# Attention, two expert layers on one core: pooled v is put into its blocks by TensorE in place of on-chip transfers

## The chip, the cores and the metric

One core of a Trainium2 chip runs the whole program. The metric is the device time of one execution in microseconds (us). The profile is one further execution of the same program, with its own time.

## What is computed

The reference, cut to what matters here:

```python
batch, n_heads, seq, head_dim = (8, 8, 576, 64)        # q, k, v: [8, 8, 576, 64]

def _attn_ref(q, k, v):
    pool = 8
    Sp = S // pool                                      # 72 pooled rows
    k_p = k.reshape(B, H, Sp, pool, D).mean(axis=3)
    v_p = v.reshape(B, H, Sp, pool, D).mean(axis=3)
    scores = scale * np.matmul(q, k_p.transpose(0, 1, 3, 2))
    scores = scores - np.max(scores, axis=-1, keepdims=True)
    attn = np.exp(scores)
    attn = attn / (np.sum(attn, axis=-1, keepdims=True) + 1e-09)
    return np.matmul(attn, v_p)

x = attn_out.transpose(0, 2, 1, 3).reshape(B * S, H * D)   # 4608 tokens of 512
x = _moe_ref(x=x, **moe_kwargs)      # the best of 8 experts for each token, 512 -> 1024 -> 512
return _moe2_ref(x=x, **moe2_kwargs) # RMS norm, gated layer 512 -> 1536 -> 512
```

## The kernel before

The program has three parts, one after the other: the attention, the expert layer in slots of 256 tokens, and the gated layer. The change lies in the attention alone.

**Tiles.** The 4608 queries are cut into 36 tiles of 128 rows: four groups (`m`) of nine. In a group the tiles 0 to 3 belong to batch 2m, 4 to 7 to batch 2m+1, and the ninth, the mixed tile, takes the last 64 queries of both. For each tile `n` of the loop at the end of the quoted code the same five steps are written out: `emit_pt(n)` turns the exponentials of the scores with TensorE (line 384, tile `pt`) and ScalarE copies them to `ptsb` (L386); `emit_qt(n + 3)` turns the queries (L348, `pq`, copied by ScalarE to `qt`); `emit_sc(n + 2)` multiplies them with the pooled keys `kbd` (L360, `sc`) and VectorE takes the maximum and subtracts; `emit_av(n)` multiplies with the pooled values (L394 or L402, `av`), VectorE divides into the output tile `x` (L421, L423), and SyncE stores it to DRAM (L426, `x_d`). The pool of output tiles, `x_p`, has three buffers, so tile n writes the buffer of tile n - 3, whose store must have landed.

**Two forms of the last product.** Tiles listed in `PLAIN` use the pooled values as they lie, in `vau`: 72 pooled rows, 8 heads of 73 columns (64 values, a one for the sum, 8 router logits). Each head needs a turn of 72 columns and a product of 73 columns, eight of each. The other tiles use blocks, `vbd`: the 4 x 72 rows of four heads are cut into three pieces of 96 rows, each with the two heads that meet in it side by side (146 columns). That is six turns and six products a tile.

**Filling the blocks.** For every batch `rows_v` and `prep_vg` fill `vau` (ScalarE L287, VectorE L322). Then `place_v` copies it into the three buffers of `vbd` in turn with six transfers from SBUF to SBUF on SyncE's queue (L330), 48 in all. Everything outside the blocks' filled cells is zero and was cleared once by GpSimd at the start (L692).

**What sets the order.** Each engine runs its instructions in the order written. The table `ORDER` and the list `E1` say at which tile, and at which of the places "a" to "e" between the five steps, a load, a pooling step or a placement stands. All plain transfers are issued by SyncE, in order: loads of q, k and v, stores of x, placements, and from tile 25 on the first expert's weights (`st`, L158 and L161), which ScalarE casts (L143) between the copies of the tiles. The build gives the transfers eight completion counters in turn, so each waits for the eighth before it to land. Loads take their buffers from a ring of 36 (`wtile`), and so does `ptsb` in a `PLAIN` tile. GpSimd pools (L241, L242 for k, L265 to L267 for v) and scatters the routing order (`ord_d`, L478).

Of the kernel before, what the change touches and what calls it, by code (L numbers as in the profile page):

```python
# [9 lines left out]
F32 = mybir.dt.float32  # L10
# [10 lines left out]
NP = 72  # L21
# [32 lines left out]

CW = [19, 30, 35, 35, 47]

PLAIN = (0, 1, 2, 3, 4, 5, 6, 9)


C_ID, C_IE, C_OFF, C_P, C_PK, C_TRI, C_TOK, C_END = 0, 128, 136, 144, 147, 211, 339, 375  # L60
# [21 lines left out]
def fused(ctx: ExitStack, tc: tile.TileContext, q, k, v, moe_w_gate, moe_w1, moe_w2,  # L82
          w_gate, w_val, w_out, rms_g, cst, out):
    nc = tc.nc
# [14 lines left out]
    ident = cc[:, C_ID:C_ID + 128]  # L99
# [39 lines left out]
    def wtile(dt, name):  # L139
        return wp.tile([128, 1024], dt, tag="w", name=name)  # L140
# [38 lines left out]
    ps = rctx.enter_context(tc.tile_pool(name="ps_a", bufs=1, space=PSUM))  # L179
    actx = ExitStack()  # L180
# [4 lines left out]
    at4 = actx.enter_context(tc.tile_pool(name="at4", bufs=1))  # L185
    at_p = actx.enter_context(tc.tile_pool(name="at", bufs=2))
    kv1 = actx.enter_context(tc.tile_pool(name="kv1", bufs=1))
    x_p = actx.enter_context(tc.tile_pool(name="xo", bufs=3))

    kbd = [at4.tile([128, 4, 2, NP], F32, name=f"kbd{i}") for i in range(3)]  # L190
    vbd = [at4.tile([96, 2, 3, 146], F32, name=f"vbd{i}") for i in range(3)]
    vau = [at4.tile([NP, H, 73], F32, name=f"vau{i}") for i in range(2)]
    lgs = sm1.tile([128, 36, E], F32, name="lgs")

# [128 lines left out]

    def place_v(b):

        va, vb = vau[b % 2], vbd[b % 3]
        v4 = va.rearrange("s (g h) n -> s g h n", g=2)
        for h, c, side, p0, s0, n in ((0, 0, 0, 0, 0, 72), (1, 0, 1, 72, 0, 24), (1, 1, 0, 0, 24, 48),
                                      (2, 1, 1, 48, 0, 48), (2, 2, 0, 0, 48, 24), (3, 2, 1, 24, 0, 72)):
            nc.sync.dma_start(out=vb[p0:p0 + n, :, c, 73 * side:73 * side + 73], in_=v4[s0:s0 + n, :, h])  # L330

    def tiles_of(m):
        return [(m, i) for i in range(9)]
# [42 lines left out]
    def emit_pt(n):  # L376
        pe = pes.pop(n).rearrange("p a h s -> p (a h s)")
        pt = [pa.tile([128, 4, 128], F32, tag=f"p{g}", name="pt") for g in range(2)]
        if n in PLAIN:
            sb, np_, nb = wtile(F32, "ptsb").rearrange("p (g c t) -> p g c t", g=2, c=4), NP, 4  # L380
# [8 lines left out]
    def emit_av(n, between=None):  # L389
        m, i = tl[n]  # L390
        sb = pts.pop(n)
        av = pav.tile([128, 2, 512], F32, tag="av", name="av")
        for h in range(H) if n in PLAIN else ():
            nc.tensor.matmul(av[:, h // 4, 73 * (h % 4):73 * (h % 4) + 73], lhsT=sb[0:NP, h // 4, h % 4],  # L394
                             rhs=vau[(2 * m + i // 4) % 2][:, h])
        for g in range(2) if n not in PLAIN else ():

# [209 lines left out]
    for name, soon, later in ORDER:  # L607
        for m in range(1, 4):
            i = soon if m == 1 else later
            plan(9 * (m - 1) + i // 5, "abcde"[i % 5], lambda f=steps[name[:-1]], b=2 * m + int(name[-1]): f(b))  # L610
    for i, w, f, x in ((E1[0], 0, sum_rows, ("k", 1, 2, nc.vector)), (E1[1], 0, sum_rows, ("k", 1, 3, nc.vector)),
                       (E1[2], 0, place_v, (0,)), (E1[3], 0, rows_k, (1,)),
                       (E1[4], 0, sum_rows, ("v", 1, 2, nc.vector)), (E1[5], 0, sum_rows, ("v", 1, 3, nc.vector)),
                       (E1[6], 0, rows_v, (1,)), (E1[7], 0, prep_vg, (1,)),
                       (E1[8], 0, place_v, (1,)), (E1[9], 0, prep_k, (GB,))):
        plan(i // 5, "abcde"[i % 5], lambda f=f, x=x: f(*x))
# [71 lines left out]
    sum_rows("v", 0, 3, nc.gpsimd)  # L688
    for z in range(2):
        nc.vector.tensor_copy(out=wg[64 * z:64 * z + 64, :, z], in_=wgl[64 * z:64 * z + 64])  # L690
    for t in kbd[1:] + vbd:
        nc.gpsimd.memset(t, 0.0)  # L692
    emit_qt(1)
    keep_warm(3)
# [348 lines left out]
    for s in range(SURE):  # L1043
# [11 lines left out]
        a = unit_steps(s, 0)  # L1055
# [169 lines left out]
```

## Time and profile before

| | us |
|---|---|
| median of 3 runs | 1744.29 (1741.7 to 1753.03) |
| the profiled execution | 1744.8 |
| span of its instructions | 1743.0 |
| the attention's tiles, about | 40 to 276 of the span |
| expert layer, about | 276 to 820 |
| gated layer, about | 820 to 1743 |

TensorE is busy 94% of the span and its mean granted clock is 0.965. The two later parts are nearly full of matmuls; the gaps are in the attention. The page's chain that ended last reaches back only to 814 us, and so says nothing of the part that is changed; for that part the waits and the order of time are read.

### The profile page before, as it was taken

To read this page: it belongs to the slowest core of one execution; us is meant where nothing else is said; L and a number is where in the kernel's file an instruction comes from. 1 tells how busy PE (TensorE), PEld (TensorE's weight loads), DVE (VectorE), ACT (ScalarE), POOL (GpSimd) and SP (SyncE) were. 2 spreads that over 40 slices of the span, in tenths; PEclk is the share of its full clock that TensorE was granted. 3 is DMA by queue.
4 is the path that set the end of the run, shared out by engine and by line. 5 is a ranking of instruction groups with operands and counts; after the bars stand their busy time and mean duration, and the time that the engine had idled before them with its cause. 6 is when DMAs were issued, how large, how long until landed. Compare 5 with 4: busy or idle time off the path is not lost.

```text
span 1743.0 us, 31176 instructions
## 1 busy us (share of the span) xinstructions
PE 1630.7 (94%) x11306; PEld 1497.9 (86%) x11307; DVE 874.7 (50%) x2087; ACT 522.6 (30%) x1186; POOL 428.1 (25%) x470
## 2 busy tenths in 40 slices
PE   7967777999899998998999999999999999999998
PEld 5867766888788887898999999999999999999997
DVE  5756765678865768522434333334433333443322
ACT  2433341243432444322222222222222222222211
POOL 5654554455643536211200000000000000000000
PEclk8877888999999999999999999999999999999999
DMA  9987872557763754313700000000000000000000
GB/s 184 237 138 172 157 124 81 195 164 237 240 197 122 244 171 164 105 37 130 271 9 19 25 26 25 25 8 18 25 25 25 25 25 7 19 25 13 13 13 13
DMA packets 116881, 163.51 MB, mean 94 GB/s; under 512 B 51280, under 2 KB 70864, under 8 KB 116704
## 3 DMA queue, kind: packets, MB, share of 16 engines
q1 hardware_dynamic: 104992, 125.38, 26.8%
q0 software_dynamic: 11712, 35.91, 6.1%
q8 instruction: 94, 1.54, 0.4%
q14 instruction: 83, 0.68, 0.1%
HBM read 116.85 MB, written 43.06 MB: 92 GB/s over the span
## 4 chain that ended last, share of the span: by engine, by line
PE 50%; DMA 2%; issue 1%; POOL 0%; POOLq 0%; ACT 0%
PE g L1131 11%; PE g L1132 11%; PE g L1130 11%; PE po L1152 6%; PE po L1153 6%; PE po L1151 6%; DMA rl<-scr 1%; PE px L1011 1%; DMA rh<-scr 1%; DMA out_dram<-o,tk 0%; POOL rh L1100 0%; POOL rl L1100 0%; POOLq L1219 0%; ACT o L1154 0%; POOLq L1100 0%
## 5 line engine op out<-in xcount | busy, mean ns | idle before, releaser
L1131 PE MATMUL g<-xl,rh 128*128 128x256 f32 x1088 | 303.0, 278 | 0.0
L1132 PE MATMUL g<-xh,rl 128*128 128x256 f32 x1088 | 302.9, 278 | 0.0
L1130 PE MATMUL g<-xh,rh 128*128 128x256 f32 x1088 | 302.7, 278 | 0.0
L1155 POOL DMA_INDIRECT out_dram<-o,tk x36 | 34.8, 968 | 792.1 <-ACT o L1154 709.2
L1131 PEld LDWEIGHTS g<-xl,rh 128*128 128x128 f32 x1088 | 204.3, 188 | 0.0
L1130 PEld LDWEIGHTS g<-xh,rh 128*128 128x128 f32 x1088 | 204.1, 188 | 0.0
L1132 PEld LDWEIGHTS g<-xh,rl 128*128 128x128 f32 x1088 | 204.0, 187 | 0.0
L493 PE MATMUL p<-xh,w1h 128*128 128x256 f32 x672 | 191.7, 285 | 8.1 <-DVE hl L498 6.1
L494 PE MATMUL p<-xl,w1h 128*128 128x256 f32 x672 | 190.0, 283 | 0.7 <-DVE xl L530 0.7
L495 PE MATMUL p<-xh,w1l 128*128 128x256 f32 x672 | 189.6, 282 | 0.0
L1135 DVE SCALAR_TENSOR_TENSOR th<-th,g 128x256 f32<-128x256 f32 x216 | 91.0, 421 | 192.5 <-ACT th L1134 191.5
L1016 DVE SCALAR_TENSOR_TENSOR xl<-px,gt,xh 128x256 fp32r<-128x256 f32 x68 | 31.4, 482 | 263.5 <-ACT xh L1015 263.5
L1130 PE MATMUL g<-xh,uh 128*128 128x256 f32 x544 | 152.7, 281 | 0.0
L1131 PE MATMUL g<-xl,uh 128*128 128x256 f32 x544 | 151.5, 278 | 0.0
L1132 PE MATMUL g<-xh,ul 128*128 128x256 f32 x544 | 151.5, 278 | 0.0
L143 ACT CAST ah<-th 128x256 fp32r<-128x256 f32 x216 | 87.9, 407 | 203.5 <-DVE th L1136 203.5
L1134 ACT ACTIVATE th<-g 128x256 f32<-128x256 f32 x216 | 82.8, 383 | 207.4 <-PE g L1132 207.4
L144 DVE TENSOR_TENSOR al<-th,ah 128x256 fp32r<-128x256 f32 x216 | 92.0, 426 | 102.2 <-ACT ah L143 101.7
L1152 PE MATMUL po<-rl,ah 128*128 128x512 f32 x360 | 142.3, 395 | 0.1
L1151 PE MATMUL po<-rh,ah 128*128 128x512 f32 x360 | 142.2, 395 | 0.0
L1153 PE MATMUL po<-rh,al 128*128 128x512 f32 x360 | 142.2, 395 | 0.0
L493 PEld LDWEIGHTS p<-xh,w1h 128*128 128x128 f32 x672 | 127.7, 190 | 13.1 <-DVE hl L498 7.3
(259 smaller groups left out, 3607.0 us busy)
## 6 DMA issues: line engine op xcount, KB each, us to landing
st<-in_moe_w_dram SPq DMA_DIRECT2D x64, 512.0 KB
y_d<-ys SPq DMA_DIRECT2D x39, 256.5 KB
y<-y_d SPq DMA_DIRECT2D x18, 513.0 KB
v<-in_v_dram SPq DMA_DIRECT2D x32, 288.0 KB
x_d<-x SPq DMA_DIRECT2D x32, 260.0 KB
q<-in_q_dram SPq DMA_DIRECT2D x32, 256.0 KB
scr<-uh SPq DMA_DIRECT2D x13, 512.0 KB
scr<-ul SPq DMA_DIRECT2D x13, 512.0 KB
```

What stands on the lines that cost most here:

```text
L143: nc.scalar.copy(out=hi, in_=src)
L144: eng.tensor_tensor(out=lo, in0=src, in1=hi, op=ALU.subtract)
L493: nc.tensor.matmul(a, lhsT=w1h[d][:, fs], rhs=xh[:, d], start=d == 0, stop=False)
L494: nc.tensor.matmul(a, lhsT=w1h[d][:, fs], rhs=xl[:, d], start=False, stop=False)
L495: nc.tensor.matmul(a, lhsT=w1l[d][:, fs], rhs=xh[:, d], start=False, stop=d == 3)
L1130: nc.tensor.matmul(g[:, j], lhsT=wh[:, sl], rhs=hi[:, d], start=d == 0, stop=False)
L1131: nc.tensor.matmul(g[:, j], lhsT=wh[:, sl], rhs=lo[:, d], start=False, stop=False)
L1132: nc.tensor.matmul(g[:, j], lhsT=wl[:, sl], rhs=hi[:, d], start=False, stop=d == 3)
L1135: nc.vector.scalar_tensor_tensor(out=th, in0=th, scalar=1.0, in1=g[:, 0], op0=ALU.add, op1=ALU.mult)
L1151: nc.tensor.matmul(po, lhsT=ah[:, tsl], rhs=wh[:, sl], start=c == 0, stop=False)
L1152: nc.tensor.matmul(po, lhsT=ah[:, tsl], rhs=wl[:, sl], start=False, stop=False)
L1153: nc.tensor.matmul(po, lhsT=al[:, tsl], rhs=wh[:, sl], start=False, stop=c == NC2 - 1)
```

## The change

`place_v` no longer issues transfers. A constant `band` of 72 x 216 holds an identity in its middle third and zeros left and right of it; a slice of 96 of its columns, taken at an offset, is an identity shifted by that offset and cut off at the block's edge. Six products of such a slice with two heads' columns of `vau` (146 columns) give all six quarter blocks, three in a PSUM tile with the tag of `pp` and three in one with the tag of `pq`, and two copies on ScalarE write both to `vbd`, all cells of it. The two tags have one buffer each and are shared with the other small products (`pp`) and the turned queries (`pq`). GpSimd clears and fills `band` and no longer clears `vbd`. The output tiles get five buffers. Of the tiles 2, 3, 5, 6 and 9, which were `PLAIN`, all five now use the blocks.

```diff
-PLAIN = (0, 1, 2, 3, 4, 5, 6, 9)
+PLAIN = (0, 1, 4)
...
-    x_p = actx.enter_context(tc.tile_pool(name="xo", bufs=3))
+    x_p = actx.enter_context(tc.tile_pool(name="xo", bufs=5))
...
+    band = at4.tile([NP, 216], F32, name="band")
...
     def place_v(b):
 
+
         va, vb = vau[b % 2], vbd[b % 3]
-        v4 = va.rearrange("s (g h) n -> s g h n", g=2)
-        for h, c, side, p0, s0, n in ((0, 0, 0, 0, 0, 72), (1, 0, 1, 72, 0, 24), (1, 1, 0, 0, 24, 48),
-                                      (2, 1, 1, 48, 0, 48), (2, 2, 0, 0, 48, 24), (3, 2, 1, 24, 0, 72)):
-            nc.sync.dma_start(out=vb[p0:p0 + n, :, c, 73 * side:73 * side + 73], in_=v4[s0:s0 + n, :, h])
+        v4 = va.rearrange("s (g h) n -> s h g n", g=2)
+        to = ((0, 0), (1, 72), (1, -24), (2, 48), (2, -48), (3, 24))
+        for a in range(2):
+            pp = ps.tile([96, 3, 2, 73], F32, tag=("pp", "pq")[a], name="pv")
+            for i, (h, by) in enumerate(to[3 * a:3 * a + 3]):
+                nc.tensor.matmul(pp[:, i], lhsT=band[:, NP - by:NP - by + 96], rhs=v4[:, h])
+            nc.scalar.copy(out=vb.rearrange("p g c (i n) -> p (c i) g n", i=2)[:, 3 * a:3 * a + 3], in_=pp)
...
-    for t in kbd[1:] + vbd:
+    nc.gpsimd.memset(band, 0.0)
+    nc.gpsimd.tensor_copy(out=band[:, NP:2 * NP], in_=ident[0:NP, 0:NP])
+    for t in kbd[1:]:
         nc.gpsimd.memset(t, 0.0)
```

TensorE's order at tile 13, where batch 4 is placed, before (`pt` the turned exponentials, `pq` the turned queries, `pvg` the logit columns of v, `sc` the scores, `av` the last product):

```order
L384 MATMUL pt<-cc,pe 96x128 x6
L348 MATMUL pq<-cc,q_556 128x128 x4
L321 MATMUL pvg<-wg,vt 72x16 x4
L360 MATMUL sc<-kbd_122,qt 128x144 x4
L402 MATMUL av<-vbd_125,ptsb 128x146 x6
L384 MATMUL pt<-cc,pe 96x128 x6
L348 MATMUL pq<-cc,mxq 128x128 x4
```

And the same place after the change, where lines are some five to seven higher (`pv` is the placement):

```order
L389 MATMUL pt<-cc,pe 96x128 x6
L353 MATMUL pq<-cc,q_554 128x128 x4
L322 MATMUL pvg<-wg,vt 72x16 x4
L365 MATMUL sc<-kbd_122,qt 128x144 x4
L407 MATMUL av<-vbd_125,ptsb 128x146 x6
L334 MATMUL pv<-vau_129,band 96x146 x6
L389 MATMUL pt<-cc,pe 96x128 x6
L353 MATMUL pq<-cc,mxq 128x128 x4
```

The six placing products stand between one tile's last product and the next tile's first turn; nothing else moved there.

SyncE's queue around the placement of batch 2, before, with what each transfer waits for (DMAHW0 to 7 are the eight counters, taken in turn):

```order
L426 DMA x_d<-x 128x520 [waits DMAHW4_49,DVE_49]
L201 DMA k_910<-in_k_dram 128x4x256 [waits DMAHW5_49,Pool_49]
L201 DMA k_912<-in_k_dram 128x4x256 [waits DMAHW6_49,Pool_49]
L330 DMA vbd_127<-vau_128 72x2x73 [waits DMAHW7_49,Activation_49]
L330 DMA vbd_127<-vau_128 24x2x73 [waits DMAHW0_49]
L330 DMA vbd_127<-vau_128 48x2x73 [waits DMAHW1_49]
L330 DMA vbd_127<-vau_128 48x2x73 [waits DMAHW2_49]
L330 DMA vbd_127<-vau_128 24x2x73 [waits DMAHW3_49]
L330 DMA vbd_127<-vau_128 72x2x73 [waits DMAHW4_49]
L218 DMA mxq<-in_q_dram 64x8x64 [waits DMAHW5_49,PE_49]
```

And after:

```order
L431 DMA x_d<-x 128x520 [waits DMAHW0_49,DVE_49]
L202 DMA k_902<-in_k_dram 128x4x256 [waits DMAHW1_49,PE_49]
L202 DMA k_904<-in_k_dram 128x4x256 [waits DMAHW2_49]
L219 DMA mxq<-in_q_dram 64x8x64 [waits DMAHW3_49,PE_49]
L219 DMA mxq<-in_q_dram 64x8x64 [waits DMAHW4_49]
```

The load of the mixed queries follows the keys at once, and the counters that it waits for belong to other transfers.

## Rows read from the trace of the kernel before

**Rows 1.** Stages: PE, PEld, DVE, ACT, POOL busy; granted clock, DMA share, GB/s.

```profile
40.00:86.00 46.00, 41.72 (x351) 40.07 (x351) 36.44 (x86) 20.93 (x43) 31.25 (x41) 0.89 0.91 232
86.00:276.00 190.00, 136.32 (x1023) 128.92 (x1023) 120.37 (x358) 67.39 (x134) 102.03 (x131) 0.82 0.74 140
```

**Rows 2.** Who TensorE waited for, 40 to 276: us, times, longest.

```profile
PE av L402 <- DMA vbd<-vau: 12.4, 3, 8.3
PE av L402 <- ACT ptsb L386: 7.5, 3, 4.0
PE av L402 <- DVE x L423: 7.3, 1, 7.3
PE pk L299 <- POOL sk L242: 6.3, 3, 4.0
```

**Rows 3.** TensorE in order of time: start, us; the waits at the blocks.

```profile
98.54 0.82 PE L402 MATMUL av<-vbd,ptsb 96*128 96x146 f32 x2 [8.33 <-DMA vbd<-vau]
...
107.27 1.00 PE L299 MATMUL pk<-cc,sk 128*128 128x64 f32 x8
...
240.09 2.31 PE L402 MATMUL av<-vbd,ptsb 96*128 96x146 f32 x8 [1.92 <-DMA vbd<-vau]
```

**Rows 4.** SyncE's queue in order of time, at two of the eight placements.

```profile
81.40 14.57 SPq L330 DMA_DIRECT2D vbd<-vau  x6
...
225.14 9.83 SPq L330 DMA_DIRECT2D vbd<-vau  x6
235.35 0.40 SPq L161 DMA_DIRECT2D st<-in_moe_w_dram  x1
```

**Rows 5.** What SyncE's queue waited for, 0 to 290: us, times, longest.

```profile
SPq L330 <- DMA x_d<-x: 7.3, 1, 7.3
```

**Rows 6.** All transfers of the placements: ns min/median/max of SyncE's instruction.

```profile
L330 SPq DMA_DIRECT2D vbd<-vau x48: 595/820/1318, 45.0 to 233.7; - x48
```

**Rows 7.** All transfers from 0 to 290: packets, bytes, sizes.

```profile
DMA packets 67175, 45.74 MB, mean 158 GB/s; under 512 B 46784, under 2 KB 55104, under 8 KB 67152
```

**Rows 8.** TensorE in order of time: turns and last products of single tiles.

```profile
83.02 1.04 PE L384 MATMUL pt<-cc,pe 128*72 128x128 f32 x8
...
85.31 1.90 PE L394 MATMUL av<-vau,ptsb 72*128 72x73 f32 x16
...
87.30 0.82 PE L384 MATMUL pt<-cc,pe 128*96 128x128 f32 x6
...
111.91 1.66 PE L402 MATMUL av<-vbd,ptsb 96*128 96x146 f32 x12
...
132.08 3.26 PE L402 MATMUL av<-vbd,ptsb 96*128 96x146 f32 x12 [4.52 <-DVE x L421]
```

**Rows 9.** ScalarE's copies from PSUM, 40 to 276, by shape: busy us, mean ns.

```profile
L386 ACT COPY ptsb<-pt 96x384 f32<-96x384 f32 x56 | 24.8, 475 | 70.1 <-PE pt L384 58.4 <-PE pq L348 4.0 <-PE sc L360 2.8
...
L350 ACT COPY qt<-pq 128x512 f32<-128x512 f32 x31 | 17.8, 575 | 3.4 <-PE pq L348 3.0 <-PE sc L360 0.4
```

**Rows 10.** GpSimd in order of time: end of pooling k for batch 4; the first tokens' gather; pooling for batch 7.

```profile
99.48 0.72 POOL L242 TENSOR_TENSOR sk<-k 128x256 f32<-128x256 f32 x1
...
199.55 0.99 POOL L571 DMA_INDIRECT tok<-ord_d,i  x1 [6.08 <-DVE rs L409]
...
205.20 0.73 POOL L242 TENSOR_TENSOR sk<-k 128x256 f32<-128x256 f32 x1
```

**Rows 11.** VectorE in order of time: an output tile that waited for a store.

```profile
131.24 0.69 DVE L421 TENSOR_TENSOR x<-av,rs 128x512 f32<-128x512 f32 x1 [4.88 <-DMA x_d<-x]
```

**Rows 12.** ScalarE in order of time: casts of the first expert's weights that waited for their load.

```profile
235.35 1.04 ACT L143 CAST w1h<-st 128x1024 fp32r<-128x1024 f32 x1 [6.95 <-DMA st<-in_moe_w_dram]
243.62 1.05 ACT L143 CAST w2h<-st 128x1024 fp32r<-128x1024 f32 x1 [5.41 <-DMA st<-in_moe_w_dram]
```

**Rows 13.** TensorE in order of time: the logit columns of batch 4.

```profile
114.76 0.63 PE L321 MATMUL pvg<-wg,vt 128*72 128x16 f32 x8
```

**Rows 14.** VectorE in order of time: those columns' copy into `vau`.

```profile
118.70 0.22 DVE L322 COPY vau<-pvg 72x64 f32<-72x64 f32 x1 [2.48 <-remote]
```

## Prediction

> **What bounds the kernel now.** First the table of stages: from 40 to 86 us TensorE is busy 41.7 of 46 us, from 86 to 276 only 136.3 of 190 us, at a mean granted clock of 0.82, while the transfers' engines are busy 0.74 of the time [rows 1]. So in the second stretch neither is full: 53.7 us of TensorE's time are waits. The list of waits then names them: 12.4 us on the transfers that fill the blocks, 7.5 us on ScalarE's copy `ptsb`, 7.3 us on an output tile, 6.3 us on pooled keys [rows 2]. Third, in order of time, the two places where the blocks are awaited, 98.5 and 240.1 us [rows 3], and SyncE's queue at the same places, where six transfers hold it for 14.6 and 9.8 us [rows 4]. In the first, 7.3 us of this are a wait for an earlier store [rows 5], since every transfer waits for the eighth before it. After 276 us the program is nearly full of matmuls and the change touches nothing there; it only starts earlier or later, so what is won or lost before 276 is won or lost at the end.
>
> What a wait costs is not its length alone. After one, TensorE runs slowly: the twelve halves of the last product took 3.26 us behind a wait of 4.5 us, 1.66 us without one [rows 8], close to the ratio of the two levels, 1.2 and 2.4 GHz. With the turn that follows I count 2.5 us behind each long wait.
>
> **The change part by part.**
>
> *The wait at batch 2's blocks.* It goes: TensorE need not stand at 98.5. What is late next is the product on the pooled keys of batch 4 (L299), which ran at 107.3 [rows 3]. GpSimd had those keys ready only at 99.5 + 0.7 = 100.2 [rows 10], and their load stands on SyncE ahead of the placement, so it does not come sooner. TensorE can come to that product at about 100.2 where it came at 107.3: a gain of 7.1 us. The new products of batches 2 and 3, and the dearer ones of tile 9, stand in front of this wait and are hidden in it.
>
> *Output tiles.* With three buffers VectorE waited 4.9 us for a store at tile 14 [rows 11], and TensorE behind it 4.5 us [rows 8]; at 195 it waited for the output tile 7.3 us [rows 2]. With five buffers the store in question is two tiles older. A tile takes over 4 us even when nothing waits (turn 0.82 and last product 1.66 alone are 2.5 [rows 8]), so two tiles cover both waits. That is 4.5 + 7.3 = 11.8, and two slow restarts at 2.5 us: 16.8. But at the second place another wait takes over: GpSimd pools the keys of batch 7 behind the first tokens' gather, which starts at 199.55 and has to see the scatters landed; the keys are ready at 205.9 [rows 10]. If the gather cannot move by more than about half of what TensorE gains there, some 6 us come back as a wait for pooled keys. I take 11 us, with 5 and 17 as ends.
>
> *The end of the attention.* Here ScalarE waits for the first expert's weights, 7.0 us at 235 and 5.4 us at 243.6 [rows 12], and TensorE waits for the copies queued behind those casts, part of the 7.5 us [rows 2]. The load of the fifth piece goes out at 235.35, straight behind the placement that held SyncE from 225.1 [rows 4]. Without it that load can go 10 us sooner. The wait at 235 is for an earlier piece and stays. Of the other I take the 1.9 us at the blocks [rows 3], 3 us of the copies' waits, and one slow restart of 2.5: 7 us, with 2 and 12 as ends.
>
> *New work on TensorE.* Six products of 96 columns against 146 are nearest to the last product's six of the same width: 1.66 us a batch at the higher clock, 3.26 at the lower [rows 8]; 13.3 us for eight, 26.1 at most. Against that five tiles take the blocks' form, which saves 1.04 - 0.82 in turns and 1.90 - 1.66 in products [rows 8], 0.46 us each, 2.3 in all. Of the eight placements those of batches 2 and 3 lie in the wait above; batch 5's comes at tile 19, ahead of a wait for queries, and batch 7's ahead of the weights' wait at 235 [rows 12]. Batches 0 and 1 fall in the dense stretch before 86, where they cost 3.3 us, less 1.8 for four of the tiles. On the path I count batches 0, 1, 4 and 6: 6.6 - 2.3 = 4.3 us.
>
> *New waits on TensorE.* The placement needs the logit columns in `vau`, from VectorE, and both single PSUM buffers. Nothing like it is in this trace. Batch 4's columns were done on TensorE at 115.4 and copied by VectorE only at 118.7 [rows 13, 14]; the scores and a last product, some 3 us, stand in between in the new order. Below, a wait of zero, above, 3 us each. The two copies on ScalarE are 438 columns of 96 rows, between the rows for 384 and 512 columns: 0.5 us each [rows 9]. The next turn of queries waits for the second, behind 0.8 us of other turns. I take 0.4 us for each of the four placements on the path: 1.6 us. ScalarE is busy 67 of 190 us [rows 1] and bears 8 us more. No gain below zero is possible in this term, as it only adds.
>
> *SyncE and GpSimd.* 48 instructions of 0.82 us [rows 6], 39 us, leave SyncE's queue. What stood behind them are loads and stores, so they go out sooner, but only part is ever awaited; beyond the places above I count nothing. GpSimd clears less at the start, where nothing waits for it.
>
> *The transfers' engines.* The placements are 288 rows times two groups times eight batches, 4608 pieces of 292 bytes: 6.9% of the 67175 packets up to 290 us, and 1.35 MB, 2.9% of the bytes [rows 7]. Busy share times length is 182 us between 40 and 276 [rows 1]; by packets they held 12.6 us of it, by bytes 5.3. The Trainium skill (DMA: Bandwidth & Descriptors, section "Why small descriptors are slow (HBM only)") says that transfers between SBUF and SBUF do not pay the penalty of small pieces; by it the smaller figure holds, and the removal relieves the loads by less than the count of packets suggests. No row here separates the two. The sum counts neither, since the engines are not full in that stretch; it matters for the third rival.
>
> **Sum.** 7.1 + 11 + 7 = 25.1 gained, 4.3 + 1.6 = 5.9 paid: 19 us less. The profiled execution took 1744.8 us (span 1743.0 and 1.8 around it), half a microsecond over the median of the runs, 1744.29. 1744.3 - 19 = 1725.
>
> **Rivals.**
>
> *The loads refill the gaps.* If the attention goes at the pace at which q, k and v land, TensorE comes earlier to the next load and waits there. Then only the waits at the blocks and one restart are won, about 12.4 + 2.5, and half comes back: 1737. For it speaks a transfer share of 0.91 before 86 [rows 1]; against it 0.74 after.
>
> *The queue was the pace.* If the eight counters, six of them taken by each placement, held the loads back, they now run ahead and most of TensorE's 53.7 us go. Two thirds of it, 36 us: 1708. For it speaks the store that a placement waited for [rows 5]; against it that only two of eight placements were awaited [rows 3]. The rule of the Trainium skill (that page and section) would make it a little less likely; the chance is given without it.
>
> *Slower: the placement stands in TensorE's queue.* A transfer waited for VectorE on the side; now everything behind the products waits too. If VectorE's copy comes as late as in rows 13 and 14, each of the eight placements costs 1.66 to 3.26 plus some 3 us, at 6 us each 48, against 2.3 saved, 12.4 of the blocks and 11.8 of the output tiles: 1744.3 + 21.5 = 1766. It decides from 26.5 / 8 = 3.3 us a placement. Against it: between the columns and the placement stand other products, and half the placements lie in front of other waits.
>
> **How the numbers follow.** Chances: the forecast (1717 to 1733) 0.46, refilled gaps 0.23, the queue 0.18, slower 0.13. About 1% is what a measurement of this kernel can tell from no change, 17.4 us: faster lies under 1726.9. Of the forecast six parts in ten lie there, with the queue's case 0.46; within 1% lie the rest of the forecast, the refilled gaps and a little of the slower case, 0.43; slower 0.11. The range leaves out most of the slower case and the lower end of the queue's: 1707 to 1746.
>
> **What would show it.** No wait of `av` on `vbd` beyond a microsecond, and at tile 10 a wait for pooled keys in its place; no wait of VectorE for `x_d`; the load behind batch 7's placement some 10 us sooner against its tile; placements of 1.7 us without a gap in front. TensorE's waits in the attention should fall from 58 us (4.3 and 53.7 in the two stretches [rows 1]) to about 40. It is wrong if TensorE stands in front of `pv`, if waits for q, k and v grow by what the others lost, or if they vanish with them.

## Result and profile after

| | before | after |
|---|---|---|
| median of 4 runs, us | 1744.87 (1741.70 to 1753.03) | 1724.07 (1723.67 to 1731.15) |
| the profiled execution, us | 1744.8 | 1731.15 |
| span of its instructions, us | 1743.0 | 1729.1 |

The ratio is 0.9886, with a 95% interval from 0.9850 to 0.9923: 20.8 us less between the medians, and the interval lies wholly below one. The profiled execution of after is the longest of its four runs, by 7 us; the other three lie between 1723.67 and 1724.44. Its times are therefore read against each other, and the medians carry the size.

The stages of after, with TensorE, its weight loads, VectorE, ScalarE and GpSimd busy, the granted clock, the transfers' share and GB/s, answer to [rows 1]:

```profile
40.00:86.00 46.00, 39.22 (x275) 37.96 (x274) 32.52 (x71) 16.72 (x36) 29.65 (x38) 0.76 0.85 222
86.00:276.00 190.00, 158.27 (x1228) 148.49 (x1227) 139.94 (x404) 78.23 (x159) 105.92 (x137) 0.89 0.73 142
```

In the long stretch TensorE is busy 158.3 us where it was 136.3, at a clock of 0.89 where it was 0.82; its last 20 us belong to the expert layer in after. Its waits there are 31.7 us (53.7 before), and in both stretches together 6.8 + 31.7 = 38.5 (58 before). In the short stretch it did less work than before, at a lower clock. Where the attention ends is read from its last product, first in before and then in after (start, length, in order of time):

```profile
266.89 1.72 PE L405 MATMUL av<-vbd,ptsb 96*64 96x146 f32 x24
```

```profile
253.69 1.72 PE L410 MATMUL av<-vbd,ptsb 96*64 96x146 f32 x24
```

It comes 13.2 us sooner, and the span is 13.9 us shorter: what follows takes 1743.0 - 266.9 = 1476.1 and 1729.1 - 253.7 = 1475.4 us. All but 0.7 us of this pair's gain lies in the attention.

Who TensorE waited for in after, 40 to 276 us (us in total, times, longest), answers to [rows 2]:

```profile
PE op__3089 L820 <- DVE ogf L817: 7.1, 1, 7.1
PE pk L300 <- POOL sk L243: 6.2, 2, 5.3
PE av L407 <- ACT ptsb L391: 5.7, 2, 4.8
PE pv L334 <- DVE vau L323: 4.8, 3, 3.6
PE sc L365 <- DVE kbd L316: 3.5, 1, 3.5
```

The wait for the blocks (12.4) and the two for an output tile (7.3 us [rows 2], 4.5 us [rows 8]) are gone. The first row belongs to the expert layer, which now begins inside the window. New is the fourth: the placement waits for the copy of the logit columns.

TensorE in order of time (idle before it in brackets): the placement of batch 3 and the keys' product behind it, two later placements, and the last long wait, answering to [rows 3]:

```profile
103.73 1.73 PE L334 MATMUL pv<-vau,band 72*96 72x146 f32 x12 [0.63 <-DVE vau L323]
...
107.55 1.00 PE L300 MATMUL pk<-cc,sk 128*128 128x64 f32 x8
...
119.32 1.66 PE L334 MATMUL pv<-vau,band 72*96 72x146 f32 x12
...
211.45 3.23 PE L334 MATMUL pv<-vau,band 72*96 72x146 f32 x12 [3.63 <-DVE vau L323]
236.10 3.29 PE L407 MATMUL av<-vbd,ptsb 96*128 96x146 f32 x12 [4.82 <-ACT ptsb L391]
```

The placement's products and copies (ns min/median/max); each of the six products of a batch runs as two, so there are 96, and 16 copies:

```profile
L334 PE MATMUL pv<-vau,band x96: 285/286/560, 37.5 to 214.2; 72*96 72x146 f32 x96
L335 ACT COPY vbd<-pv x16: 521/522/536, 39.2 to 214.7; 96x438 f32<-96x438 f32 x16
```

SyncE's queue at the fifth piece of the first expert's weights, which stood at 235.35 behind batch 7's placement in [rows 4]:

```profile
214.49 0.33 SPq L431 DMA_DIRECT2D x_d<-x  x1
215.02 0.39 SPq L161 DMA_DIRECT2D st<-in_moe_w_dram  x1
```

ScalarE's casts that wait for those loads, as in [rows 12]:

```profile
225.53 1.04 ACT L143 CAST w1h<-st 128x1024 fp32r<-128x1024 f32 x1 [3.21 <-DMA st<-in_moe_w_dram]
234.63 1.04 ACT L143 CAST w2h<-st 128x1024 fp32r<-128x1024 f32 x1 [6.25 <-DMA st<-in_moe_w_dram]
```

GpSimd at the first tokens' gather and the last pooled keys of batch 7, as in [rows 10]:

```profile
184.28 0.99 POOL L576 DMA_INDIRECT tok<-ord_d,i  x1 [6.87 <-DMA ord_d<-tok,rpi]
...
189.95 0.72 POOL L243 TENSOR_TENSOR sk<-k 128x256 f32<-128x256 f32 x1
```

The gather comes 15.3 us sooner than at 199.55, and the keys are ready at 190.7; TensorE takes them at 193.5 without a wait.

### The profile page after: what moved, and what is told of

It reads as the page before. It is cut to its first block, busy times and chain, and to the rows that moved or that the text cites. A ratio compares the mean times of both kernels' runs of the same rounds, so it can differ in the third digit from the quotient of the medians.

```text
span 1729.1 us, 31214 instructions
## 1 busy us (share of the span) xinstructions
PE 1640.8 (95%) x11373; PEld 1507.4 (87%) x11373; DVE 883.4 (51%) x2087; ACT 527.8 (31%) x1202; POOL 425.9 (25%) x469
## 2 busy tenths in 40 slices
DMA packets 111632, 162.16 MB, mean 94 GB/s; under 512 B 46032, under 2 KB 65616, under 8 KB 111456
## 4 chain that ended last, share of the span: by engine, by line
PE 50%; DMA 2%; issue 1%; POOL 0%; POOLq 0%; ACT 0%
PE g L1138 11%; PE g L1139 11%; PE g L1137 11%; PE po L1159 6%; PE po L1160 6%; PE po L1158 6%; DMA rl<-scr 1%; PE px L1018 1%; DMA rh<-scr 1%; DMA out_dram<-o,tk 0%; POOL rh L1107 0%; POOL rl L1107 0%; POOLq L1226 0%; ACT o L1161 0%; POOLq L1107 0%
```

## Experiments

Not all runs were on the same chip: those below are from three, on which the kernel before had medians of 1754.57, 1757.57 and 1743.37 us. So the ratio to before on the same chip is what is compared; 1% is 17.5 us. Theory (the prediction's ledger): the gain is made of single waits, at batch 2's blocks, the output tiles and the end. Rival (the prediction's third): the placements in SyncE's queue held back everything else, and it is the queue that was relieved.

**The three parts, each alone.** First the products in place of the transfers, with three output tiles and the old list:

```diff
-PLAIN = (0, 1, 4)
+PLAIN = (0, 1, 2, 3, 4, 5, 6, 9)
-    x_p = actx.enter_context(tc.tile_pool(name="xo", bufs=5))
+    x_p = actx.enter_context(tc.tile_pool(name="xo", bufs=3))
```

> Only the placement is changed: products in place of transfers; three output tiles and the eight plain tiles stay. By the ledger of the prediction (wait at the blocks 7 us, end of the attention 7 us, less 4 to 8 us of work and waits on TensorE): 1745 less 6 to 10, that is 1735 to 1739, with waits of VectorE for stores of x still there. If the queue of transfers was the pace (third rival): 1715 or less, and the waits for x gone as well. If placing stands in TensorE's way (slower rival): above 1750.

Measured: 1736.2 us, ratio 0.9895 (0.9850 to 0.9939), 18 us less. That is nearly the whole change, and twice what the ledger gave this part. The rival's sign is there, though not its size (30 us): VectorE's waits for stores of x, 16.9 us before, are 2.8.

Then the kernel before with five output tiles only (`bufs=3` to `bufs=5`):

> Only the output tiles go from three to five. By the ledger: the two waits for stores (4.5 and 7.3 us) and two slow restarts go, about 6 us come back at the pooled keys: 1745 - 11 = 1734. If loads refill the gaps: 1740 to 1745, with TensorE's waits for q, k and v longer by what the store waits lost.

Measured: 1750.78 us, ratio 0.9972 (0.9944 to 0.9999): 5 us less, half of the ledger's 11. TensorE's waits in it, 40 to 300 us, show where the rest went:

```profile
PE av L402 <- DMA vbd<-vau: 23.1, 4, 10.0
PE pq L348 <- DMA q<-in_q_dram: 18.4, 4, 7.9
```

No wait for an output tile is among the large ones, but the one for the blocks has grown from 12.4 to 23.1 us and one for queries from 3.1 to 18.4: TensorE comes sooner to what the queue delivers late. This profiled run is the second longest of ten (1760.24), so in a run near the median the waits may be shorter.

And the kernel before with only the shorter `PLAIN`:

> Only the list of plain tiles is cut to 0, 1 and 4; transfers still place. Tiles 2, 5 and 9 now come within one to four steps of their placement. By the ledger 2.3 us saved on TensorE, and a wait for the six transfers (some 5 us of issue and their landing) at up to three tiles: 1745 to 1757. If the transfers land in time: 1742 to 1744.

Measured: 1764.43 us, ratio 1.0063 (1.0040 to 1.0087), 11 us more. The tiles that use blocks sooner stand and wait for the transfers (TensorE in order of time):

```profile
49.85 3.30 PE L402 MATMUL av<-vbd,ptsb 96*128 96x146 f32 x12 [8.34 <-DMA vbd<-vau]
71.29 3.26 PE L402 MATMUL av<-vbd,ptsb 96*128 96x146 f32 x12 [6.50 <-DMA vbd<-vau]
111.02 3.26 PE L402 MATMUL av<-vbd,ptsb 96*128 96x146 f32 x12 [12.00 <-DMA vbd<-vau]
```

Each costs twice: the wait, and 3.3 us in place of 1.7 for the product behind it.

**Two parts together.** The change with three output tiles (the second line of the first diff alone):

> The changed kernel with three output tiles. By the ledger the store waits come back: 1724 + 11 = 1735. If the placements in the queue were what delayed the stores (queue rival): 1724 to 1727, with waits for x under 2 us in all.

Measured: 1732.57 us, ratio 0.9867 (0.9825 to 0.9909), and TensorE waits 0.5 us for output tiles. Beside the products, five output tiles bring nothing that can be measured here: the ledger's 11 us would have put this kernel at 0.9949, outside its interval.

The change with the old list (the first line of that diff alone):

> The changed kernel with the old list of eight plain tiles. By the ledger 5 x 0.46 = 2.3 us more work on TensorE, part of it hidden: 1724 to 1727. If the plain tiles' five further buffers of the ring (ptsb) delay loads: 1728 or more, with longer waits for k, q or v in the first third.

Measured: 1736.35 us, ratio 0.9859 (0.9809 to 0.9908), the same as the change within the intervals. With products the form of the five tiles is worth too little to see. Against the products alone (0.9895) this kernel also prices five output tiles: 0.0036, 6 us, with intervals that overlap by far, so some microseconds for them stay possible.

Five output tiles and the shorter list, but with the transfers:

> Five output tiles and three plain tiles, but transfers still place: what the products themselves bring is the difference to the changed kernel. By the ledger 1724 + 7 + 7 - 6 = 1732, plus waits for the blocks at tiles 2, 5 and 9: 1732 to 1742. If the queue was the pace: 1745 or more.

Measured: 1767.52 us, ratio 1.0063 (1.0042 to 1.0085), no better than the list alone; TensorE waits 31.2 us for the blocks. Without the products the other two parts together lose 11 us.

**What the transfers cost when nobody waits for them.** The kernel with three output tiles and products, and besides them the old six transfers per batch into a tile that nothing reads:

```diff
+    vdump = at4.tile([96, 2, 3, 146], F32, name="vdump")
...
+            nc.sync.dma_start(out=vdump[p0:p0 + n, :, c, 73 * side:73 * side + 73], in_=v6[s0:s0 + n, :, h])
```

> The changed kernel with three output tiles, and beside the products the old six transfers a batch still go out, into a tile that nobody reads. Against the changed kernel with three output tiles it prices the transfers' place in SyncE's queue and on the engines alone, without any wait for blocks. By the ledger (only the load at the end of the attention is delayed): 3 to 10 us more. If the queue was the pace: 15 us more or above. If transfers between SBUF are cheap and the queue has room: within 2 us.

Measured: 1752.04 us, ratio 0.9973 (0.9942 to 1.0005): 0.0106 above the kernel without them, 18.6 us, as much as the products gained; by the two intervals, some 9 us either way. In its trace no instruction of TensorE, VectorE, ScalarE or GpSimd waits for these transfers. TensorE's waits in it, 40 to 276 us:

```profile
PE pk L301 <- POOL sk L244: 9.6, 5, 5.0
PE av L412 <- ACT ptsb L396: 9.3, 4, 5.8
PE av L412 <- DVE x L431: 8.6, 4, 6.9
```

These are 27.5 us; without the idle transfers the same three are 6.6, 2.6 and 0.2, 9.4 us. So it is not the blocks: it is pooled keys, the copies behind the weights' casts, and output tiles that wait for their stores, and SyncE's queue issues the loads or stores behind all three.

**Count, or bytes?** The same kernel with each of the six cut to one row, then with one transfer of the whole `vau` in their place:

```diff
-            nc.sync.dma_start(out=vdump[p0:p0 + n, :, c, 73 * side:73 * side + 73], in_=v6[s0:s0 + n, :, h])
+            nc.sync.dma_start(out=vdump[p0:p0 + 1, :, c, 73 * side:73 * side + 73], in_=v6[s0:s0 + 1, :, h])
```

> The changed kernel with three output tiles and with the old six transfers per batch into a tile that nobody reads, each cut to one partition's row (two pieces of 292 bytes instead of 48 to 144): the same 48 instructions in SyncE's queue, the same counters and waits on the copy of v, almost no bytes. The output is unchanged. With whole transfers this kernel stood at a ratio of 0.9973, without any at 0.9867, some 18.6 us of difference. Theory A, the price is in the queue (48 issues that wait for the copy of v, and what stands behind them): it stays, ratio 0.995 to 0.998, +14 to +19 us over the kernel without them. Theory B, the price is the packets and bytes on the sixteen DMA engines: it goes, ratio 0.986 to 0.988, within 3 us of the kernel without them.

Measured: 1731.87 us, ratio 0.9944 (0.9916 to 0.9972), just under what theory A gave.

```diff
+        nc.sync.dma_start(out=vdump, in_=va)
```

> The same kernel with one transfer per batch of the whole copied v (72 partitions x 584 numbers, the bytes of the old six together, in 72 longer packets) into a tile that nobody reads: 8 instructions in SyncE's queue instead of 48, each with the same wait for VectorE's copy. The output is unchanged. Theory A1, the number of instructions in the queue is the price: a sixth of 18.6 us stays, about 3 us, ratio 0.988 to 0.989. Theory A2, the wait of the queue for the copy of v is the price, whatever stands behind it: most stays, ratio 0.994 to 0.997. Theory B1, the bytes: most stays as well. B2, the number of packets: a twelfth stays, ratio 0.987 to 0.988. Together with the kernel of tiny transfers the four part: count (tiny dear, one cheap), wait (both dear), bytes (tiny cheap, one dear), packets (both cheap).

Measured: 1725.59 us, ratio 0.9910 (0.9880 to 0.9941), between what A1 and A2 gave. SyncE's queue shows the difference, at batches 1 and 2; six small ones first, then one large one:

```profile
62.53 6.54 SPq L340 DMA_DIRECT2D vdump<-vau  x6
...
80.55 11.29 SPq L340 DMA_DIRECT2D vdump<-vau  x6
```

```profile
63.20 2.38 SPq L337 DMA_DIRECT2D vdump<-vau  x1
...
84.82 0.79 SPq L337 DMA_DIRECT2D vdump<-vau  x1
```

Over all eight places the tiny ones held the queue 46.3 us, nearly as long as the whole ones of the idle transfers (50.7) and those in before (55.9), the large ones 9.3. What waits behind the queue follows. VectorE's waits for a store of x and GpSimd's for a load of v, up to 290 us, with six whole transfers, six tiny ones, one large one and none:

```profile
DVE x L431 <- DMA x_d<-x: 14.2, 5, 6.5
POOL v L267 <- DMA v<-in_v_dram: 31.5, 6, 11.9
```

```profile
DVE x L431 <- DMA x_d<-x: 9.0, 4, 5.8
POOL v L267 <- DMA v<-in_v_dram: 27.6, 6, 10.6
```

```profile
DVE x L428 <- DMA x_d<-x: 4.9, 1, 4.9
POOL v L267 <- DMA v<-in_v_dram: 11.0, 4, 5.5
```

```profile
DVE x L426 <- DMA x_d<-x: 2.9, 1, 2.9
POOL v L266 <- DMA v<-in_v_dram: 9.3, 4, 3.5
```

The tiny ones add 193 packets and 0.03 MB to the kernel without any, the large ones 672 and 1.34, the whole ones 5249 and 1.35: in these traces the two waits go with the number of instructions, not with the bytes. In time, six transfers almost without bytes keep 0.0077 of the 0.0106, 13 us, and their interval lies just clear of the kernel without any. The price thus hangs mostly on instructions in the queue with their counters. One transfer keeps 0.0043, 7.5 us, and its interval overlaps both neighbours: whether a part of the price is the bytes, or the queue's wait for the copy of v, stays open. The profiled execution of the tiny ones was among the shortest of its six runs (1726.85 of 1726.43 to 1739.78), so its trace shows which waits came back and not all that the others lost; the size rests on the ratios.

**The price of the products.** Each placing product twice:

```diff
-                nc.tensor.matmul(pp[:, i], lhsT=band[:, NP - by:NP - by + 96], rhs=v4[:, h])
+                for _ in range(2):
+                    nc.tensor.matmul(pp[:, i], lhsT=band[:, NP - by:NP - by + 96], rhs=v4[:, h])
```

> The changed kernel with every placing product done twice: 8 x 1.6 us more on TensorE in the same places. By the ledger about half the placements lie before other waits: 1724 + 6 = 1730 (4 to 9 more). If TensorE's queue is the pace all through the attention: 13 us more or above. If loads are: within 2 us.

Measured: 1741.59 us, ratio 0.9924 (0.9879 to 0.9970), 0.0038 above the change: 6.6 us for some 13 us of added work. That is what the ledger's half on the path gives, but the intervals overlap: the difference is uncertain by 10 us, so neither none nor all 13 can be excluded.

**Stores issued later.** In after, SyncE's longest waits are for VectorE at the stores: 130.3 us over all rows where it was 63.7, with 53.2 and 14.7 in the largest. Would it help to let the loads pass? The store of each tile is held back by one tile's turn, then by two:

```diff
-            nc.sync.dma_start(
-                out=x_d[b * S:b * S + 512, :].rearrange("(p r) d -> p r d", r=4)[:, i % 4], in_=xf)
+        held_x.append((m, i, xf))
+        if len(held_x) > LATE or n == NTL - 1:
+            store_x(NTL if n == NTL - 1 else 1)
```

> The changed kernel with the store of each output tile issued one tile's turn later on SyncE, so that the loads behind it in the queue do not wait for VectorE's sum (in the changed kernel SyncE waited 53.2 us there, the longest 10.4 us). If the queue still sets the pace of attention: faster than the changed kernel by 3 to 12 us, ratio 0.98 to 0.985. If the loads are no longer what attention waits for: no change, ratio 0.987 to 0.99. If the stores that come later hold up the gathers behind attention, which read what they store: slower by 2 to 5 us, ratio 0.99 to 0.992.

Measured: 1723.53 us, ratio 0.9884 (0.9854 to 0.9914).

> The same with each store issued two tiles' turns later. If the queue sets the pace: as with one turn or up to 4 us better, ratio 0.978 to 0.985, unless the five tiles' buffers run out, which would show as a wait of VectorE for a store. If loads are not awaited: ratio 0.987 to 0.99. If the gathers are held up: 0.99 to 0.994.

Measured: 1722.15 us, ratio 0.9886 (0.9857 to 0.9914). Neither differs from the change, within some 8 us either way: to let the loads pass a store by one or two tiles brings nothing that can be measured. SyncE still waits 122.7 and 101.3 us at the stores in the two traces, so the queue was put in another order and not emptied. No kernel here is faster than the change beyond the intervals. The second one's runs spread widely, 1709.76 to 1726.50, and its profiled run is the shortest; its stage from 40 to 86 us and the attention's last product:

```profile
40.00:86.00 46.00, 36.53 (x305) 34.09 (x303) 35.84 (x77) 18.78 (x41) 30.66 (x41) 0.93 0.99 230
```

```profile
236.83 1.72 PE L412 MATMUL av<-vbd,ptsb 96*64 96x146 f32 x24
```

Here the granted clock is 0.93 in the stage in which the profiled run of after had 0.76, and the attention ends 16.9 us sooner, though the ratios of the two kernels are the same. Two single profiles thus differ by 21.4 us (1731.15 and 1709.76), as much as the change is worth: they show where waits stand, and not what a change brings.

## Why the prediction was right in its total and wrong in its parts

Forecast 1725 us, measured 1724.07. That the two agree to a microsecond is luck: two terms, 7.1 and 11 us, are not found where the sum put them, and most of the gain came from the queue, 18.6 us, of which the sum had only the 7 us at the end. TensorE's waits fell to 38.5 us, where about 40 was said; 7.1 of them belong to the expert layer.

*The wait at batch 2's blocks, 7.1 us.* The wait is gone, as said, but in the profiled run of after nothing is won by it. No wait for pooled keys stands at tile 10: the product on the keys of batch 4 runs at 107.55, where it ran at 107.27 [rows 3]. TensorE reached batch 3's keys 12 us later than before (94.0 against 82.1), with a clock of 0.76 in that stretch and three placements, 6.8 us, ahead of it; and the keys themselves came later, at 106.0 in place of 100.2, since SyncE issued their load at 90.2 and not at 80.3. In the products kernel of the first experiment, with a clock of 0.85 there, the wait that the step named is found:

```profile
100.95 0.56 PE L300 MATMUL pk<-cc,sk 128*128 128x64 f32 x4
102.58 0.66 PE L300 MATMUL pk<-cc,sk 128*128 128x64 f32 x4 [1.07 <-POOL sk L243]
```

The product ends at 103.2 there and at 108.3 in before, 5 us sooner. In the kernel with stores two tiles late the keys were ready at 90.8, the clock was 0.93, and the product still came at 103.74. So the mechanism is seen in some kernels and not in others, the 7.1 us in none of these three, and the step "it does not come sooner" should have left room for later.

*Output tiles, 11 us.* Here the step failed. Five tiles alone are worth 5 us, and beside the products nothing that can be measured. The waits for x were real, but their cause was the store held up in the queue by placements, not the number of tiles alone: with the transfers away TensorE's fall to 0.5 us with three tiles, and with idle transfers they come back (8.6 us). One wait, two ways to be rid of it, and the sum credited the second and left the first at nothing. The 6 us expected back behind the gather did not come, because the gather's scatters moved with the rest.

*The end, 7 us.* The fifth piece goes out 20.3 us sooner. The store ahead of the placement went out here in before:

```profile
224.71 0.33 SPq L426 DMA_DIRECT2D x_d<-x  x1
```

In after it goes out at 214.49, 10.2 us sooner, so 10.1 remain for the placement that is gone: what the prediction said. The casts still wait 3.2 and 6.3 us (7.0 and 5.4). TensorE's waits for `ptsb` at the end fall from 7.1 (4.0 and 3.1) to 5.7 and the 1.9 us at the blocks go, 3.3 in all; of two slow stretches behind such waits one stays, behind the wait at 236. With 2.5 us for the other that is 5.8, a little under the term.

*New work, 4.3 us.* The price of the work is right: the eight placements take 18.3 us in the trace, between the 13.3 and 26.1 of the prediction. Doubling them costs 6.6 us, just the warm price of the four that were put on the path, but within the noise of that run the share on the path is not settled. The list's 2.3 us are too small to be seen.

*New waits, 1.6 us.* Too small: 4.8 us at the logit columns and 1.3 at ScalarE, 6.1 over all eight, and a slow placement (3.23) behind the longest. That one, 3.6 us, has a cause that the step did not consider, told in the last section. The slower rival decided from 3.3 us a placement, work and wait together. The eight come to 24.4 us, 3.05 each and 6.9 at the longest, so its price was nearly paid. As 20.8 us were won all the same, a part of it lies off the path, or the 26.5 us that it set against it were too few. ScalarE's copies took 0.52 us (0.5).

*The queue, nothing beyond the places named.* This is the step that was wrong. 48 transfers for which nobody waits cost 18.6 us, uncertain by 9, of which the sum had only what it counted at the end; the rival named for it was right about the cause and too high in its size (36 us). The argument against it, that only two of eight placements were awaited, looked at who waits for a placement and not at who stands behind it. With products and idle transfers the kernel stands at 0.9973: what the products bring apart from the queue is some 5 us, between -1 and 10. That loads refill the gaps did not come true with products; in the kernel with five tiles and transfers one profiled run, longer than its median, shows it (18.4 us for queries).

*The transfers' engines.* The prediction left open whether small pieces cost by packets or by bytes. Tiny transfers cost most of what whole ones do, so that was a minor question: over the whole program the packets fell from 116881 to 111632 and the bytes from 163.51 to 162.16 MB, and the queue's instructions mattered more. The Trainium skill (DMA: Bandwidth & Descriptors, section "Why small descriptors are slow (HBM only)") exempts transfers between SBUF and SBUF from the penalty on small pieces; the runs do not speak against it, since whole and tiny transfers differ by 0.0029, within the intervals.

## What to carry to other kernels

A transfer's price is also what it does to the queue in which it stands: list what is issued behind it, and count a wait for a store or a load there as the same wait that a bigger pool would remove, not as a second gain. To price a transfer in a queue, leave it in with its result unused, then cut it to one row: the two runs part waiting for it, issuing it and moving its bytes. A change of data layout that needs its data early (here the blocks in early tiles) should be tried after the delivery has been made faster: alone it cost 11 us, and with products nothing that can be seen, though no gain of its own is shown either.

## What the runs showed of the hardware that was not expected

A VectorE instruction that takes 0.20 us elsewhere in after (at 101.8 and 145.7) took 5.00 while GpSimd worked. VectorE, GpSimd and VectorE again, in order of time in after:

```profile
206.27 5.00 DVE L455 TENSOR_TENSOR rob<-rcd,rcm 128x40 bf16<-128x40 f32 x1
...
206.55 4.64 POOL L144 TENSOR_TENSOR w1l<-st,w1h 128x1024 fp32r<-128x1024 f32 x2
211.19 0.21 DVE L323 COPY vau<-pvg 72x64 f32<-72x64 f32 x1
```

VectorE's small comparison ends at 211.27 and GpSimd's two subtractions at 211.19; the copy of the logit columns stands behind it, and TensorE's placement behind the copy waits 3.6 us. The Trainium skill (SBUF — State Buffer, section "SBUF: two separate sides") says that the two engines share a pair of ports which one holds for a whole instruction while the other is blocked, for VectorE's instructions with two inputs in SBUF among others. The trace agrees that VectorE was held, here until two GpSimd instructions in a row had passed. By that section whichever starts first has the ports; the recorded start of VectorE, 206.27, lies before that of GpSimd, 206.55, so in this the records do not agree. Nothing here tried the order the other way, and the cause is read from this one place.

The granted clock of the first 86 us differs between kernels in which TensorE has the same instructions there. Batch 0's placement took 3.12 us at 37.5 in after, and the products behind it ran at the lower level until about 52 us; in the kernel with stores two turns late it took 2.06 at 34.6, and the product behind it 1.90 and not 3.5. In both it had fallen to the lower level behind a wait for queries, 5.5 us in the one and 4.0 in the other; before waited 5.7 us there and was back at the higher level by 38.8. So the length of that wait alone does not decide it, and what does was not found.
